# A decode backward kernel bound by 16 DMA engines: a fourth dV tile stored by 15 engines, and three wq loads moved to GpSimd's ring

## The chip, the cores and the metric

The kernel runs on 1 core of one Trainium2 chip. The metric is the device time of one execution in microseconds (us); lower is better. The kernel before took 404.36 us (median of three runs, 404.33 to 404.38). The profiled span is about 2 us shorter than the time.

The engines are called as in the profile: PE (matmul), DVE (vector), ACT (scalar), POOL (GpSimd), SP (sync). A DMA that SP issues goes into the hardware ring (q1 in the profile), one that GpSimd issues into the software ring (q0). Both are served by the same 16 DMA engines.

## The reference, cut to what matters

The outputs are the value and all gradients of a gated mix of one attention block for one token with a K and V cache, and one small MLP. What weighs is the caches: 32 heads, each with K and V of 4096 x 128 in bf16, 1 MB each, and their gradients, which are as large.

```python
def _A_ref(x, k_cache, v_cache, wq, wo):            # D = 640, H = 32, Sk = 4096, Dh = 128
    q = (x @ wq).reshape(B, Sq, H, Dh).transpose(0, 2, 1, 3)
    scores = jnp.einsum("bhqd,bhkd->bhqk", q, k_cache) * (Dh ** -0.5)
    p = _softmax(scores, axis=-1)
    o = jnp.einsum("bhqk,bhkd->bhqd", p, v_cache)
    return o.transpose(0, 2, 1, 3).reshape(B, Sq, H * Dh) @ wo
# [...] B: x @ w1 + b1, mish, @ w2
def reference(...):
    _out, _vjp = jax.vjp(_f, A_x, A_k_cache, A_v_cache, A_wq, A_wo, B_w1, B_b1, B_w2, gate_w)
    return (_out, *_vjp(grad_out))                   # dK and dV are 32 MB each
```

## The kernel before

It goes through the heads one after the other. K and V of a head are loaded three heads ahead, through SP's ring. Each head makes one dK tile and one dV tile of 1 MB, which GpSimd stores through its ring. One row of a tile is one partition: 32 x 128 elements of bf16, 8,192 bytes.

```python
    outs = ctx.enter_context(tc.tile_pool(name="outs", bufs=5))        # dK and dV tiles share 5 buffers
    tsb = ctx.enter_context(tc.tile_pool(name="tsb", bufs=4))
    wts = ctx.enter_context(tc.tile_pool(name="wts", bufs=2))
# [...]
    def ring(h):
        return nc.sync if h >= H - 2 else nc.gpsimd

    def load_k(h):
        if h < H:
            kts[h] = kv_in.tile([P, J, Dh], BF16, name="Kn", tag="Kn", bufs=KB)
            nc.sync.dma_start(kts[h][:], Kv[h])
# [...] load_v likewise
    def load_wq(w):
        if w < H // WG:
            wqs[w] = wts.tile([P, RC, WG * Dh], BF16, name="wq_g", tag="wq_g")
            nc.sync.dma_start(wqs[w][:], wq_v[:, :, w * WG * Dh:(w + 1) * WG * Dh])

    def load_wo(g):
        if g < NG:
            wos[g] = wts.tile([P, G, D], BF16, name="wo_g", tag="wo_g", bufs=3)
            nc.sync.dma_start(wos[g][:], wo_v[g])
# [...]
        def dwo():                                   # the gradient of wo is written over wo's own buffer
            for i in range(G):
                nc.vector.tensor_scalar(wos[g][:, i, :], da_bc[:], fs["o4"][:, i:i + 1], None, ALU.mult)
            (nc.sync if g == NG - 1 else nc.gpsimd).dma_start(dwo_v[g], wos[g][:])
# [...]
        if half == 1:                                # dv_half, after the outer product on DVE
            if h in (8, 17, 26):
                spread(h // 9, dVv[h], st["dV"])
            else:
                ring(h).dma_start(dVv[h], st["dV"][:])

    def spread(i, dst, t):
        src = t[:].rearrange("p j d -> p (j d)")
        out = dst.rearrange("p j d -> p (j d)")
        if i == 0:
            nc.gpsimd.inc_swdge_sem([], [], mode="reset_dge_cursor")
        for a, b in (((120, 125), (0, 120), (125, 128)), ((0, 14), (14, 119), (119, 128)), ((0, 8), (8, 128)))[i]:
            nc.gpsimd.dma_start(out[a:b, :], src[a:b, :], max_dma_last_dim=J * Dh)
# [...]
    for h in range(H):
        hh, g = h % G, h // G
        if hh == 3:
            load_wo(g + 2)
            if g % 2 == 0:
                load_wq(g // 2 + 1)
        load_k(h + 3)
        load_v(h + 3)
        period(h)
# [...]
```

`spread` is the device that the change uses once more. A store of 128 rows takes all 16 DMA engines, 8 rows each. A store of 120 rows takes 15. The odd pieces around it are there to choose which engine the 120 rows leave out.

## Time and profile before

| | before |
|---|---|
| time | 404.36 us (404.33 to 404.38) |
| moved by DMA | 164.93 MB |
| software ring, packets of 8,192 and of 4,096 bytes | 7,296 and 768 |
| DVE, PE, ACT busy | 75%, 74%, 44% of the span |
| the last DMA, dwq_l: fifteenth and last of its 16 landings | 398.93 and 401.22 us |

The first lines are from the page of the kernel before: span; the mean busy share of the 16 DMA engines and their GB/s in 40 equal slices of the span; the packet counts; each ring with packets, MB and share of the 16 engines' span; and the engine shares of the chain of waits that ended last.

```profile
span 402.3 us, 13607 instructions
...
DMA  7999999999999999999999999999999999999984
GB/s 283 418 416 406 419 424 420 418 422 424 422 422 418 423 414 403 425 423 423 422 421 424 423 422 419 418 426 425 421 423 425 421 424 417 425 420 417 424 368 189
DMA packets 28136, 164.93 MB, mean 410 GB/s; under 512 B 3164, under 2 KB 3868, under 8 KB 12204
...
q1 hardware_dynamic: 17136, 93.41, 56.3%
q0 software_dynamic: 10880, 70.64, 42.1%
q8 instruction: 46, 0.75, 0.7%
...
DVE 40%; DMA 27%; PE 20%; issue 5%; ACT 4%; POOL 0%; ACTq 0%; SPq 0%; POOLq 0%
DMA Kn<-in_A_k_cache_dram 22%; DVE dK_sb L612 10%; DVE dV_sb L612 9%; PE tr L587 8%; DVE junk L385 5%; DMA out_dram<-wo_g 4%; ACT tT L589 4%; PE sA L667 3%; DVE junk L288 3%; PE sA L596 3%; PE sB L720 2%; DVE junk L537 2%; DVE junk L494 1%; DMA vec_rows<-in_gate_w_dram 1%; DVE wo_g L374 1%
...
```

Read the row of DMA first. It is at 9, that is 90% or more, from the second slice to the last but two, at 414 to 426 GB/s in most. Compute engines are busy for three quarters. So the DMA engines bind, and the chain of waits does not say it: it gives DVE 40% and DMA 27%, since it follows what released each instruction and not which resource was full. The bandwidth agrees with what the Trainium skill ("DMA: Bandwidth & Descriptors", Bandwidth) measured for a load of 16 MB, 425 GB/s: most 8,192-byte packets here take 309 ns, and 16 engines at that pace move 424 GB/s.

These are the lines of the page on DMA issues (transfer, issuing sequencer, count, KB each, median us from issue to landing).

```profile
...
Kn<-in_A_k_cache_dram SPq DMA_DIRECT2D x32, 1024.0 KB, 23.7
...
out_dram<-dK_sb POOLq DMA_DIRECT2D x30, 1024.0 KB, 12.1
out_dram<-dV_sb POOLq DMA_DIRECT2D x27, 1024.0 KB, 12.0
wq_g<-in_A_wq_dram SPq DMA_DIRECT2D x4, 1280.0 KB, 19.6
...
out_dram<-wo_g POOLq DMA_DIRECT2D x7, 640.0 KB, 11.5
...
```

The stores through the software ring land 12 us after issue.

This is what SP's queue waited for (us in all, times, longest). L121 is the load of K. L136 is the load of wo.

```profile
...
SPq L121 <- PE sB L720: 182.6, 23, 19.6
SPq L136 <- DMA out_dram<-wo_g: 56.1, 5, 16.4
...
```

The first line is flow control: SP waits for a K buffer. The wait costs nothing as long as the DMA engines have other work, as the row of DMA shows here. In the second line, SP waits for the store of a wo_g buffer before it may load the next wo into it, 16.4 us at most.

The next lines are windows of the kernel before: start and end, length, busy us and instruction counts of the engines, the granted TensorE clock, the DMA share and GB/s.

```profile
...
core 0: us, PE busy (x) PEld busy (x) DVE busy (x) ACT busy (x) POOL busy (x), PEclk, DMA share, GB/s
...
280.00:290.00 10.00, 8.81 (x181) 7.91 (x177) 9.71 (x24) 5.89 (x15) 1.06 (x2) 1.00 1.02 423
290.00:300.00 10.00, 8.39 (x173) 7.51 (x171) 9.81 (x22) 5.24 (x14) 1.07 (x2) 1.00 1.01 424
...
380.00:390.00 10.00, 0.72 (x2) 0.27 (x2) 7.83 (x32) 0.26 (x1) 0.00 (x0) 0.50 0.96 401
...
```

And these are the lines on the wq loads and who waited for them (us, times).

```profile
...
L131 SPq DMA_DIRECT2D wq_g<-in_A_wq_dram x4: 412/466/548, 0.7 to 242.5; - x4
...
  PEld L278: 8.3, 2
  PE qc_ps L278: 8.1, 2
...
```

Before the end, the transfers of the kernel show who is late. Each transfer raises its semaphore 16 times, once per DMA engine. The times of these landings come from the semaphore records of the trace (us from the start of the span, in order; no engine is named there):

```
dK of the last head, second half, issued 381.96:
  388.50 388.75 388.82 388.97 389.10 389.81 392.58 393.89 394.10 394.78 395.31 395.43 395.51 395.61 395.68 | 398.09
dwq_l, the last DMA of the weights, issued 393.48:
  396.58 396.60 396.62 396.63 396.65 396.67 396.75 397.14 397.34 398.03 398.56 398.66 398.77 398.86 398.93 | 401.22
```

One engine is 2.3 us behind all others. It is called the straggler below.

### The profile page before, as it was taken

To read this page: it belongs to the slowest core of one execution; us is meant where nothing else is said; L and a number is where in the kernel's file an instruction comes from. 1 tells how busy PE (TensorE), PEld (TensorE's weight loads), DVE (VectorE), ACT (ScalarE), POOL (GpSimd) and SP (SyncE) were. 2 spreads that over 40 slices of the span, in tenths; PEclk is the share of its full clock that TensorE was granted. 3 is DMA by queue.
4 is the path that set the end of the run, shared out by engine and by line. 5 is a ranking of instruction groups with operands and counts; after the bars stand their busy time and mean duration, and the time that the engine had idled before them with its cause. 6 is when DMAs were issued, how large, how long until landed. Compare 5 with 4: busy or idle time off the path is not lost.

```text
span 402.3 us, 13607 instructions
## 1 busy us (share of the span) xinstructions
PE 298.5 (74%) x5872; PEld 270.1 (67%) x5872; DVE 303.1 (75%) x791; ACT 177.4 (44%) x411; POOL 45.6 (11%) x92
## 2 busy tenths in 40 slices
PE   0688898669888788978877989719887888888200
PEld 0587787668778677868766878618776777777200
DVE  3338666646599999987669799845999997899850
ACT  1355555325454555546523556505554455545000
POOL 0001111010112111111101112100110111111000
PEclk9999999857999999989988899957999999999655
DMA  7999999999999999999999999999999999999984
GB/s 283 418 416 406 419 424 420 418 422 424 422 422 418 423 414 403 425 423 423 422 421 424 423 422 419 418 426 425 421 423 425 421 424 417 425 420 417 424 368 189
DMA packets 28136, 164.93 MB, mean 410 GB/s; under 512 B 3164, under 2 KB 3868, under 8 KB 12204
## 3 DMA queue, kind: packets, MB, share of 16 engines
q1 hardware_dynamic: 17136, 93.41, 56.3%
q0 software_dynamic: 10880, 70.64, 42.1%
q8 instruction: 46, 0.75, 0.7%
q14 instruction: 14, 0.11, 0.1%
q10 hardware_dynamic: 60, 0.01, 0.0%
HBM read 82.03 MB, written 82.03 MB: 408 GB/s over the span
## 4 chain that ended last, share of the span: by engine, by line
DVE 40%; DMA 27%; PE 20%; issue 5%; ACT 4%; POOL 0%; ACTq 0%; SPq 0%; POOLq 0%
DMA Kn<-in_A_k_cache_dram 22%; DVE dK_sb L612 10%; DVE dV_sb L612 9%; PE tr L587 8%; DVE junk L385 5%; DMA out_dram<-wo_g 4%; ACT tT L589 4%; PE sA L667 3%; DVE junk L288 3%; PE sA L596 3%; PE sB L720 2%; DVE junk L537 2%; DVE junk L494 1%; DMA vec_rows<-in_gate_w_dram 1%; DVE wo_g L374 1%
## 5 line engine op out<-in xcount | busy, mean ns | idle before, releaser
L589 ACT COPY tT<-tr 128x512 f32<-128x512 f32 x256 | 142.5, 588 | 137.7 <-PE tr L587 136.9
L596 PEld LDWEIGHTS <-tT 128*128 128x128 bf16 x2048 | 79.8, 98 | 40.1 <-ACT tT L589 34.6
L587 PE MATMUL tr<-ident_f,Kn 128*128 128x128 f32 x512 | 81.9, 298 | 12.6 <-DMA Kn<-in_A_k_cache_dram 12.6
L612 DVE TENSOR_TENSOR dV_sb<-p_bf,qd 128x2048 bf16<-128x2048 bf16 x64 | 78.0, 1218 | 0.3 <-issue 0.3
L612 DVE TENSOR_TENSOR dK_sb<-ds_bf,qd 128x2048 bf16<-128x2048 bf16 x64 | 77.6, 1214 | 0.0
L587 PE MATMUL tr<-ident_f,Vn 128*128 128x128 f32 x512 | 74.3, 281 | 0.0
L587 PEld LDWEIGHTS tr<-ident_f,Kn 128*128 128x128 f32 x512 | 61.2, 152 | 13.9 <-issue 13.9
L596 PE MATMUL sA<-qd,tT 128*128 128x48 bf16 x1024 | 48.9, 187 | 23.8 <-ACT dq_all L725 12.7
L587 PEld LDWEIGHTS tr<-ident_f,Vn 128*128 128x128 f32 x512 | 57.4, 144 | 0.0
L596 PE MATMUL sB<-qd,tT 128*128 128x48 bf16 x1024 | 46.1, 183 | 0.0
L667 PEld LDWEIGHTS <-Vn 128*128 128x128 bf16 x1024 | 30.2, 96 | 10.4 <-issue 10.4
L667 PE MATMUL sA<-e_bf,Vn 128*128 128x48 bf16 x1024 | 30.7, 183 | 7.6 <-DVE zs L687 6.0
L720 PE MATMUL sB<-ds_bf,Kn 128*128 128x48 bf16 x1024 | 32.5, 186 | 1.4 <-DVE ds_bf L709 1.4
L629 POOL DMA_DIRECT2D out_dram<-dK_sb x30 | 17.2, 574 | 143.6 <-DVE rz L689 90.1
L671 DVE TENSOR_REDUCE m<-sA 128x1 f32<-128x32 f32 x32 | 6.0, 189 | 35.2 <-PE sA L596 28.5
L720 PEld LDWEIGHTS <-Kn 128*128 128x128 bf16 x1024 | 29.8, 98 | 1.6 <-issue 1.6
L642 POOL DMA_DIRECT2D out_dram<-dV_sb x27 | 14.6, 541 | 139.4 <-DVE dV_sb L612 53.3
L288 DVE SCALAR_TENSOR_TENSOR junk<-wo_g,da_bc 128x640 bf16<-128x640 bf16 x32 | 26.2, 820 | 1.7 <-ACT da_bc L229 1.1
L385 DVE SCALAR_TENSOR_TENSOR junk<-wq_g,dq_bc 128x1024 bf16<-128x1024 bf16 (+1 forms) x25 | 25.1, 1004 | 0.2
L691 ACT ACTIVATE p_bf<-e_bf,rz 128x64 bf16<-128x64 bf16 x32 | 11.1, 348 | 13.3 <-DVE rz L689 10.6
L707 DVE TENSOR_SCALAR_CACHE_REDUCE dj<-sB,rz 128x128 f32<-128x128 f32 x32 | 11.1, 346 | 7.5 <-PE sB L701 7.5
L698 DVE SCALAR_TENSOR_TENSOR pj<-sB,e_bf 128x32 f32<-128x32 f32 x32 | 6.1, 190 | 12.6 <-PE sB L596 12.4
(152 smaller groups left out, 273.6 us busy)
## 6 DMA issues: line engine op xcount, KB each, us to landing
Kn<-in_A_k_cache_dram SPq DMA_DIRECT2D x32, 1024.0 KB, 23.7
Vn<-in_A_v_cache_dram SPq DMA_DIRECT2D x32, 1024.0 KB, 28.2
out_dram<-dK_sb POOLq DMA_DIRECT2D x30, 1024.0 KB, 12.1
out_dram<-dV_sb POOLq DMA_DIRECT2D x27, 1024.0 KB, 12.0
wq_g<-in_A_wq_dram SPq DMA_DIRECT2D x4, 1280.0 KB, 19.6
wo_g<-in_A_wo_dram SPq DMA_DIRECT2D x8, 640.0 KB, 11.4
out_dram<-wo_g POOLq DMA_DIRECT2D x7, 640.0 KB, 11.5
out_dram<-dwq_t SPq DMA_DIRECT2D x4, 896.0 KB, 18.4
```

The source lines that it names most:

```text
L288: nc.vector.scalar_tensor_tensor(junk[:, 0:D], in0=wos[g][:, i, :], scalar=1.0, in1=da_bc[:], op0=ALU.mult, op1=ALU.mult, accum_out=gp["do ...
L385: nc.vector.scalar_tensor_tensor(junk[:, c0:c1], in0=wqs[w][:, rc, c0:c1], scalar=1.0, in1=dq_bc[:, w * WG * Dh + c0:w * WG * Dh + c1], op ...
L587: nc.tensor.transpose(tp[:, t, :], flat[:, k * P:(k + 1) * P], ident_f[:])
L589: nc.scalar.copy(sb[:].rearrange("p a b -> p (a b)"), tp[:].rearrange("p a b -> p (a b)"))
L596: nc.tensor.matmul(out[:, 2 * k:2 * k + W], lhsT=tb[:, t, par, :], rhs=vec[:, par, :].unsqueeze(1).to_broadcast([P, W // 2, 2]), start=(pa ...
L612: nc.vector.tensor_tensor(dst[:, a:b, :].rearrange("p j (a b) -> p j a b", b=2), col[:, a:b, :].unsqueeze(2).to_broadcast([P, n, Dh // 2, 2]),
L629: ring(h).dma_start(dKv[h], st["dK"][:])
L642: ring(h).dma_start(dVv[h], st["dV"][:])
L667: nc.tensor.matmul(O, lhsT=vts[h][:, j, :], rhs=st["e"][:, j:j + 1].to_broadcast([P, W]), start=(j == 0), stop=(j == J - 1))
L691: nc.scalar.activation(p_bf[:], e[:].unsqueeze(2).to_broadcast([P, J, 2]), ACT.Copy, scale=rz[:])
L707: nc.vector.tensor_scalar(dj[:], PT, rz[:], None, ALU.mult, ALU.add, accum_out=dd[:])
L720: nc.tensor.matmul(DQ, lhsT=kts[h][:, j, :], rhs=ds[:, j, 0:1].to_broadcast([P, W]), start=(j == 0), stop=(j == J - 1))
```

## The change

The intent: take one more dV tile off the slowest DMA engine (four spread tiles for three), and move three wq loads of 1.25 MB from SP's ring, where K and V queue behind them, to GpSimd's.

```diff
     def load_wq(w):
         if w < H // WG:
             wqs[w] = wts.tile([P, RC, WG * Dh], BF16, name="wq_g", tag="wq_g")
-            nc.sync.dma_start(wqs[w][:], wq_v[:, :, w * WG * Dh:(w + 1) * WG * Dh])
+            (nc.gpsimd if w else nc.sync).dma_start(wqs[w][:], wq_v[:, :, w * WG * Dh:(w + 1) * WG * Dh])
@@ dv_half
-            if h in (8, 17, 26):
-                spread(h // 9, dVv[h], st["dV"])
+            if h % 7 == 5 and h < H - 3:
+                spread(h // 7, dVv[h], st["dV"])
@@ spread
-        if i == 0:
+        if i % 3 == 0:
             nc.gpsimd.inc_swdge_sem([], [], mode="reset_dge_cursor")
-        for a, b in (((120, 125), (0, 120), (125, 128)), ((0, 14), (14, 119), (119, 128)), ((0, 8), (8, 128)))[i]:
+        for a, b in (((120, 125), (0, 120), (125, 128)), ((0, 14), (14, 119), (119, 128)), ((0, 8), (8, 128)))[i % 3]:
```

The spread tiles are now those of heads 5, 12, 19 and 26.

## The prediction

> **What bounds the kernel.** The 16 DMA engines. The 40-slice view has 420 to 425 GB/s in most slices; the table of windows gives a DMA share of 1.01 to 1.03 from 10 to 380 us. The page counts 164.93 MB; an 8,192-byte packet takes 309 ns, so 16 engines move 424 GB/s and need 389 us. Compute ends at 388.8 us, the span at 402.3.
>
> **Which engine.** The semaphore records show 16 landings per transfer, which show one engine's lag without its name. One is alone at the end: the last dK half lands at 388.5 (first), 394.1 (ninth), 395.7 (fifteenth) and 398.1 us (last); dwq_l at 396.6, 397.3, 398.9 and 401.2. Instruction fetch (46 packets of 16 KB, about 1 us each, one every 7 to 8 us) looks like its burden. Spread stores already relieve it: before the third (328 us) it is 4.3 to 4.8 us behind the fifteenth, after it 1.7.
>
> The Trainium skill ("DMA: Bandwidth & Descriptors", Why a DMA increments its semaphore by 16 and not by 1) says a software-ring transfer uses the largest k up to 16 that divides its partitions, on consecutive engines from a cursor. By that, 120 rows take 15 engines, and the pieces 5/120/3, 14/105/9, 8/120 all skip engine 4 with their big piece. The packet counts of before agree with the pieces (768 packets of 4,096 bytes for three tiles); no view names the engine.
>
> **What the change does.**
> 1. Four spread tiles (heads 5, 12, 19, 26) for three (8, 17, 26). The added one is of the 5/120/3 form: engine 4 carries 2 rows for 8, estimate 8 x 309 - 4 x 159 = 1.8 us less. Engines that get 9 rows in 4,096-byte packets gain 18 x 159 - 8 x 309 = 0.4 us. Two more issues on GpSimd (0.6 us each, 11% busy) and a cursor reset (18 ns): nothing.
> 2. Three wq loads (1.25 MB each) move from SP's ring to GpSimd's. Bytes, packets (640 of 2,048 bytes) and engines stay; the same page ("Issuing engines are not separate DMA queues") says rings share the 16 engines. Effects: K and V behind them on SP's ring come about 3 us earlier (1.25 MB at 424 GB/s), and wq itself lands after perhaps 12 to 15 us instead of 19.6 (dK and dV take 12 there), which should shorten PE's waits for wq (8.1 us in two). Neither is critical: the DMA engines have a backlog there.
>
> **Critical path.** Only the straggler's 1.8 us. Its last landing goes from 401.2 to about 399.4; the fifteenth goes from 398.9 to 399.0 to 399.3: they nearly meet. wo_g and dwq_l, issued at 391.3 and 393.5 after landings of the straggler (dwq_t at 393.4), go out about 2 us earlier. Time: 404.36 - 1.9 = 402.4 us; 401.2 to 403.8. Faster by over 2% (under 396.3): 0.02; within: 0.97; slower: 0.01.
>
> **Right if:** bytes and GB/s in mid-run unchanged; 1,024 packets of 4,096 bytes on the software ring instead of 768; gap of last to fifteenth landing at the end under 1 us instead of 2.3; PE's wait for wq falls.
>
> **Wrong if:** another engine is the straggler, or the cursor stands elsewhere (no gain, or 1 to 2 us slower); wq's 640 rows through software descriptors delay the stores behind them; the straggler had idle time, so that relief isn't time; ring order changes what waits at the end.

## The result, and the profile after

The changed kernel took 403.12 us (median of five runs: 403.73, 402.78, 402.68, 403.12, 403.42). The kernel before, five runs on the same chip, took 404.15 to 404.38. The ratio is 0.9974, with a 95% interval of 0.996 to 0.9988. (A ratio is the mean time of one kernel's runs over the mean of the other's in the same rounds, so it is not quite the ratio of the quoted medians.) The gain is about 1.05 us of the 1.9 predicted. The profiled run was the slowest of the five, 403.73 us.

The page of the changed kernel, the same lines:

```profile
span 401.8 us, 13610 instructions
...
DMA  8999999999999999999999999999999999999995
GB/s 285 420 415 399 420 423 408 423 422 421 417 415 425 423 422 412 423 424 420 423 419 422 424 421 422 414 422 425 415 399 423 421 422 420 424 421 416 423 410 213
DMA packets 27400, 164.93 MB, mean 410 GB/s; under 512 B 3260, under 2 KB 3964, under 8 KB 11596
...
q1 hardware_dynamic: 15168, 89.48, 54.0%
q0 software_dynamic: 12112, 74.57, 44.7%
q8 instruction: 46, 0.75, 0.7%
...
DVE 42%; DMA 25%; PE 19%; ACT 6%; issue 4%; POOL 0%; ACTq 0%; DVEq 0%; POOLq 0%
DVE dK_sb L612 11%; DVE dV_sb L612 9%; DMA out_dram<-dV_sb 9%; DMA out_dram<-dK_sb 8%; DMA wq_g<-in_A_wq_dram 7%; PE tr L587 6%; DVE junk L385 5%; ACT tT L589 5%; PE sA L667 4%; DVE junk L288 3%; PE sA L596 3%; PE sB L720 2%; DVE wo_g L374 1%; DMA vec_rows<-in_gate_w_dram 1%; DVE dj L707 1%
...
```

The bytes and the mean of 410 GB/s are as before. Two things differ. The last slices carry more (410 and 213 GB/s for 368 and 189): the engines end closer together. One slice in the middle, the thirtieth, at 291 to 301 us, fell to 399. The shares of the chain of waits changed much (K loads with 22% have gone, dV and dK stores with 17% have come) while the time hardly moved: it names other waits, no other limit. The ring counts fit the edit: q1 lost 1,968 packets, three loads of 640 and 48 semaphore writes; q0 gained 1,232, which are 960 for wq (320 each), 128 for the tile whose 128 rows now go in two packets each, and 144 of 4 bytes (48 semaphore writes of wq and 96 of the tile, explained below).

```profile
...
Kn<-in_A_k_cache_dram SPq DMA_DIRECT2D x32, 1024.0 KB, 21.2
...
out_dram<-dK_sb POOLq DMA_DIRECT2D x30, 1024.0 KB, 18.9
out_dram<-dV_sb POOLq DMA_DIRECT2D x26, 1024.0 KB, 18.9
...
out_dram<-wo_g POOLq DMA_DIRECT2D x7, 640.0 KB, 20.1
wq_g<-in_A_wq_dram POOLq DMA_DIRECT2D x3, 1280.0 KB, 27.1
...
```

The stores of whole dK and dV tiles and of wo_g through the software ring now land 19 to 20 us after issue, not 12. The three moved wq loads took 19.7, 27.1 and 29.5 us (semaphore records), for 37.0, 19.6 and 24.1 before: on the whole neither sooner nor later.

```profile
...
SPq L121 <- PE sB L720: 138.6, 18, 16.5
SPq L136 <- DMA out_dram<-wo_g: 106.0, 5, 24.8
...
```

SP's queue waits twice as long for wo's store buffer: 106.0 us, longest 24.8. The store in the longest wait was issued at 273.1 us and landed at 293.3. The third wq load, issued at 230.2, had landed at 259.7 by then; the store stood in the software ring behind dK and dV stores that were late themselves.

```profile
...
280.00:290.00 10.00, 5.32 (x105) 4.77 (x105) 8.01 (x20) 3.69 (x11) 0.87 (x3) 0.96 1.01 422
290.00:300.00 10.00, 9.17 (x141) 8.64 (x139) 8.36 (x19) 3.94 (x9) 0.85 (x2) 0.69 0.97 390
...
380.00:390.00 10.00, 0.72 (x2) 0.27 (x2) 7.83 (x32) 0.26 (x1) 0.00 (x0) 0.50 1.01 424
...
```

From 290 to 300 us the DMA engines moved 390 GB/s for 424 before: a hole of about 0.3 MB (34 GB/s x 10 us), about 0.8 us of all 16 engines. In the last window shown they moved 424 for 401.

```profile
...
L131 POOL DMA_DIRECT2D wq_g<-in_A_wq_dram x3: 901/901/901, 50.0 to 230.2; - x3
...
  PEld L278: 6.0, 2
  PE qc_ps L278: 5.8, 2
...
```

PE's wait for wq fell from 8.1 to 5.8 us. (GpSimd waited for wq too: the same view has one wait of 8.2 us at L531 and one of 7.1 us at L629 that ended with a wq load.) K and V, which no longer stand behind wq, land sooner after issue, as the page's first line on issues shows for K: 21.2 us for 23.7. The landings at the end, from the semaphore records:

```
dwq_l, issued 392.83:
  396.01 396.02 396.02 396.05 396.06 396.16 396.40 397.85 398.00 399.04 399.13 399.25 399.27 399.30 399.56 | 400.56
```

The straggler is now 1.0 us behind the fifteenth, as intended, and the fifteenth is 0.6 us later than before.

### Following each packet to its engine

The profile has one record for every packet, with ring, size, start and end, but names no engine. The engine can be worked out: on one engine the record of a packet starts 3 to 4 ns before that of the packet before it ends, each ring is served in order, and every transfer has to end with 16 landings at known times. Chaining all 28,000 packets this way gives 16 chains. Where two engines switch in the same nanosecond two chains can be swapped, so single packets are uncertain. The straggler's chain is not, since the spread stores mark it.

What marks it is this: an engine that a piece leaves out still gets packets, of 4 bytes and 9 ns each, as many as each engine that takes part has data packets. The page itself can be used to confirm it: each spread row goes as two packets of 4,096 bytes. By the rule of the Trainium skill ("DMA: Bandwidth & Descriptors", Why a DMA increments its semaphore by 16 and not by 1), 5, 120 and 3 rows take 5, 15 and 3 engines, with 2, 16 and 2 data packets each. That is 11 x 2 + 1 x 16 + 13 x 2 = 64 filler packets, and two more DMAs with 16 semaphore packets each are 32: 96 small packets for one such tile. The same sum gives 64 for the form 14/105/9 and 48 for 8/120. The page's count of packets under 512 bytes says 3,164 with three tiles, 3,260 with four (+96), 2,956 with none (-208 = 96 + 64 + 48), and 3,372 with six (+208): exact each time. So the rule holds in this trace.

In the kernel before, exactly one chain has runs of 18, 16 and 18 such small packets in a row at the three spread tiles. It moved 9.918 MB, the others 10.08 to 10.11 (the sums leave out some 2.7 MB of the two rings, about what moved in the first 10 us), and it is the one that ended last, at 400.88 us. By the same rule it is engine 4, if the reset puts the cursor at engine 0. No run here shows that it does, so the number is a name given by this assumption; that the pieces all leave out one and the same engine, and that this engine is the last one, is what the chains show. In the changed kernel it has runs of 18, 16, 18 and 18.

| straggler, us | packets at their usual length | longer than usual | gaps | its last packet ends |
|---|---|---|---|---|
| before | 378.3 | 18.8 | 0.7 | 400.9 |
| after | 376.1 | 20.1 | 0.7 | 400.2 |

"Usual length" is 309, 196 and 159 ns for 8,192, 5,120 and 4,096 bytes. All other engines are longer than usual by 1 to 4 us in sum before and 3 to 6 after. The straggler has nearly no gaps: it works all the time, and about one in four of its packets of 8,192 bytes takes 335 to 384 ns, loads and stores alike, while those of most other engines stay at 309.

### The profile page after: what moved, and what is told of

Its sections match the earlier page's. It is cut to its first block, busy times and chain, and to the rows that moved or that the text cites. A ratio compares the mean times of both kernels' runs of the same rounds, so it can differ in the third digit from the quotient of the medians. Undisturbed runs are those within 1.5% of the kernel's fastest.

```text
span 401.8 us, 13610 instructions
## 1 busy us (share of the span) xinstructions
PE 299.1 (74%) x5872; PEld 271.2 (67%) x5872; DVE 303.1 (75%) x791; ACT 178.1 (44%) x411; POOL 49.9 (12%) x97
## 2 busy tenths in 40 slices
DMA packets 27400, 164.93 MB, mean 410 GB/s; under 512 B 3260, under 2 KB 3964, under 8 KB 11596
## 4 chain that ended last, share of the span: by engine, by line
DVE 42%; DMA 25%; PE 19%; ACT 6%; issue 4%; POOL 0%; ACTq 0%; DVEq 0%; POOLq 0%
DVE dK_sb L612 11%; DVE dV_sb L612 9%; DMA out_dram<-dV_sb 9%; DMA out_dram<-dK_sb 8%; DMA wq_g<-in_A_wq_dram 7%; PE tr L587 6%; DVE junk L385 5%; ACT tT L589 5%; PE sA L667 4%; DVE junk L288 3%; PE sA L596 3%; PE sB L720 2%; DVE wo_g L374 1%; DMA vec_rows<-in_gate_w_dram 1%; DVE dj L707 1%
## 5 line engine op out<-in xcount | busy, mean ns | idle before, releaser
L587 PE MATMUL tr<-ident_f,Kn 128*128 128x128 f32 x512 | 80.1, 293 | 0.0
L587 PE MATMUL tr<-ident_f,Vn 128*128 128x128 f32 x512 | 76.3, 286 | 0.0
L587 PEld LDWEIGHTS tr<-ident_f,Vn 128*128 128x128 f32 x512 | 59.4, 147 | 0.0
L629 POOL DMA_DIRECT2D out_dram<-dK_sb x30 | 17.2, 575 | 134.5 <-DVE rz L689 86.7
L701 PE MATMUL sB<-ident_f,part 128*128 128x128 f32 x32 | 10.5, 330 | 4.2 <-DVE pj L698 4.0
## 6 DMA issues: line engine op xcount, KB each, us to landing
Kn<-in_A_k_cache_dram SPq DMA_DIRECT2D x32, 1024.0 KB, 21.2
out_dram<-dK_sb POOLq DMA_DIRECT2D x30, 1024.0 KB, 18.9
out_dram<-dV_sb POOLq DMA_DIRECT2D x26, 1024.0 KB, 18.9
out_dram<-wo_g POOLq DMA_DIRECT2D x7, 640.0 KB, 20.1
wq_g<-in_A_wq_dram POOLq DMA_DIRECT2D x3, 1280.0 KB, 27.1
```

Of the source, the lines that this page charges most:

```text
L587: nc.tensor.transpose(tp[:, t, :], flat[:, k * P:(k + 1) * P], ident_f[:])
L629: ring(h).dma_start(dKv[h], st["dK"][:])
L701: nc.tensor.transpose(PT, part[:].to_broadcast([P, P]), ident_f[:])
```

## The experiments

Twelve kernels were run. All outputs are right. All edits are against the kernel before. Each experiment's theories are told in words beside it; a letter in an expectation stands for one of them. Runs of one call shared the runs of the kernel before: medians 404.09 (e1 to e4), 404.20 (e5 to e8), 404.19 (e9 to e11), 404.22 (e12).

| kernel | spread tiles | wq ring | median us (range) | ratio to before, 95% interval |
|---|---|---|---|---|
| before | 3 | SP | 404.1 to 404.4 | 1 |
| after | 4 | GpSimd | 403.12 (402.68 to 403.73) | 0.9974 (0.996 to 0.9988) |
| e1_four_tiles | 4 | SP | 402.89 (402.31 to 403.40) | 0.9975 (0.9963 to 0.9988) |
| e2_wq_only | 3 | GpSimd | 404.90 (404.71 to 405.02) | 1.0024 (1.0011 to 1.0036) |
| e3_no_spread | 0 | SP | 410.18 (409.84 to 410.97) | 1.0158 (1.0144 to 1.0171) |
| e4_other_engine | 3, another engine left out | SP | 411.12 (410.55 to 411.35) | 1.0176 (1.0162 to 1.019) |
| e5_five_tiles | 5 | SP | 401.98 (401.88 to 405.47) | 0.9958 (0.9933 to 0.9982) |
| e6_six_tiles | 6 | SP | 402.14 (402.01 to 402.18) | 0.9947 (0.9935 to 0.9959) |
| e7_four_tiles_other_heads | 4, other heads | SP | 402.71 (402.21 to 403.34) | 0.9963 (0.9951 to 0.9975) |
| e8_five_tiles_wq | 5 | GpSimd | 405.22 (404.49 to 406.42) | 1.0028 (1.0015 to 1.0041) |
| e9_changed_wo_late | 4, wo issued later | GpSimd | 405.80 (404.41 to 407.93) | 1.0045 (1.0022 to 1.0069) |
| e10_five_wq_wo_late | 5, wo issued later | GpSimd | 406.18 (403.94 to 406.92) | 1.0038 (1.0015 to 1.0061) |
| e11_five_wo_late | 5, wo issued later | SP | 404.91 (403.37 to 408.31) | 1.0031 (0.9997 to 1.0066) |
| e12_five_wq_wo_buffers | 5, four wo buffers | GpSimd | 404.76 (403.46 to 405.99) | 1.001 (0.9988 to 1.0032) |

### e1 and e2: each half of the change alone

The theory was that the fourth tile is the whole gain, by relief of the straggler, and the wq move is worth nothing. The rival was that the wq move has an effect of its own.

e1 has only the tile:

```diff
-            if h in (8, 17, 26):
-                spread(h // 9, dVv[h], st["dV"])
+            if h % 7 == 5 and h < H - 3:
+                spread(h // 7, dVv[h], st["dV"])
```

(with `i % 3` in `spread`, as in the change)

> Four spread tiles alone, wq loads left on SP's ring. Theories on record: R (relief): the gain is the straggling engine's lighter load, worked out as 1.8 us, and the wq move costs nothing; Q (queue): the gain comes from moving wq, the tile is neutral; RC (relief less cost): the tile gives its full 1.8 us and the wq move costs about 0.8 us of it, as dK and dV stores landed after 18.9 us instead of 12 and DVE waited for store buffers. Before is 404.3. R: 403.1 as the whole change. Q: 404.3. RC: 402.4 to 402.6, faster than the whole change; end gap of last to fifteenth landing under 1 us.

Measured: 402.89 us, ratio 0.9975. The fourth tile alone gives all that the whole change gives. The time lies between what R and RC foresaw; the gap of last to fifteenth landing was 1.50 us in the profiled run (400.53 and 399.03), not under 1.

e2 has only the wq move:

```diff
-            nc.sync.dma_start(wqs[w][:], wq_v[:, :, w * WG * Dh:(w + 1) * WG * Dh])
+            (nc.gpsimd if w else nc.sync).dma_start(wqs[w][:], wq_v[:, :, w * WG * Dh:(w + 1) * WG * Dh])
```

> The wq loads on GpSimd's ring alone, three spread tiles at heads 8, 17, 26 as before. R: 404.3, unchanged. Q: 403.1. RC: 404.8 to 405.4, slower than before by 0.5 to 1 us; wq lands after more than 20 us; dK and dV stores land after 15 to 19 us instead of 12.

Measured: 404.90 us, ratio 1.0024, its interval above 1. The move alone is a loss of 1.0 us, as RC foresaw, and the dK and dV stores landed after 20.7 to 20.8 us (15 to 19 foreseen). On top of four tiles it costs 0.2 us between the medians (403.12 and 402.89), which the runs cannot tell from nothing. Whether the move truly costs less with four tiles than with three stays open: the two intervals, of 0.0013 to 0.0014 either way, leave about 0.8 us of uncertainty in the difference between the changed kernel and e1.

### e3 and e4: is it that one engine?

e3 spreads no tile. If three spread tiles relieve the straggler by what their packets say, the kernel must lose about 6 us. e4 also cuts three dV tiles into 120 and 8 rows, but resets the cursor each time and sends the 120 rows first, so that by the rule cited above (and a reset to engine 0) another engine, engine 15, is left out. If cutting a store helped by itself, or the slow engine were 15, e4 would be as fast as before. If only relief of engine 4 helps, e4 is as slow as e3.

```diff
e3:
-            if h in (8, 17, 26):
+            if False:
e4:
-        if i == 0:
-            nc.gpsimd.inc_swdge_sem([], [], mode="reset_dge_cursor")
-        for a, b in (((120, 125), (0, 120), (125, 128)), ((0, 14), (14, 119), (119, 128)), ((0, 8), (8, 128)))[i]:
+        nc.gpsimd.inc_swdge_sem([], [], mode="reset_dge_cursor")
+        for a, b in ((0, 120), (120, 128)):
```

> Before with no spread tile at all: all dV tiles stored by all 16 engines. Relief theories (R, RC): the straggler carries 3 tiles' relief more, 1.83 + 1.83 + 2.15 = 5.8 us by packets (8 of 309 ns less its own 4 or 2 of 159 ns), so 410.1 us (409 to 411) and a last landing 6 to 8 us behind the fifteenth at the end. Q: no more than 1 us slower than before.

> Before with its three spread tiles cut as rows 0 to 120 and 120 to 128, with the cursor reset each time: by the skill's rule the big piece takes engines 0 to 14 and leaves out engine 15, and the 8 rows go to 15 and 0 to 6, so engine 4 gets 9 rows in 4,096-byte packets, 0.36 us more than a plain tile, instead of 1 or 2. If engine 4 is the straggler and the cursor rule holds: 410.1 + 1.1 = 411.2 us (410 to 412), slower even than no spread tile. If it doesn't matter which engine is spared, or the straggler is 15: 404.3 or less.

Measured: 410.18 us and 411.12 us. Relief of one certain engine is worth 6.1 us for three tiles; relief of the other one, engine 15 by the rule, is worth nothing (0.9 us slower than no cutting, which is near the scatter). The chain of the straggler has no run of fillers in either. In both, the straggler ends alone: the second dK half of the last head lands at 395.16 (fifteenth) and 404.48 (last) in e3, and at 395.24 and 404.65 in e4. The Trainium skill ("DMA: Bandwidth & Descriptors", Latency and other measured facts) says engines 7 and 15 are usually slower than the rest; here, by the same page's cursor rule and if the reset means engine 0, it is engine 4.

The chains of before and e3 also settle what does not burden the straggler. Instruction fetch (46 packets of 16 KB, about 1 us each) falls on eight other engines in turn, about six fetches each, and shows there as 5 to 6 us of gaps. The straggler's chain has 0.4 us of gaps in all, and its own packets are 19.5 us too long. So it is not the fetch.

### e5, e6 and e7: more tiles, other heads

If the straggler were the only limit, the fifth and sixth tile would each give as much as the fourth. If a second limit lies close behind, the gain ends. e7 keeps four tiles, the three of before and head 22, to see if the place of the tiles matters.

```diff
e5:
+            if h % 6 == 4 and h < H - 3:              # heads 4, 10, 16, 22, 28
+                spread(h // 6, dVv[h], st["dV"])
e6:
+            if h % 5 == 3 and h < H - 3:              # heads 3, 8, 13, 18, 23, 28
+                spread(h // 5, dVv[h], st["dV"])
e7:
+            if h in (8, 17, 22, 26):
+                spread((8, 17, 22, 26).index(h), dVv[h], st["dV"])
```

> Five spread tiles (heads 4, 10, 16, 22, 28), wq on SP's ring. Theory F (floor): the fourth tile gave 1.0 us only as its relief was over-counted (18 more 4-byte packets of 9 ns on the spared engine: 1.65 us, not 1.83) and as that engine's packets ran 0.6 us longer in sum; a fifth gives the same again until the eight engines that fetch instructions (last at 398.6 us before, 0.3 to 0.4 us more with the extra rows) are last: about 1.9 us under before, 402.0 to 402.4 if before is 404.1, spared engine no longer last by more than 0.5 us. Rival S (saturation): the fourth tile met something else that ends the program; the fifth gives nothing, 402.9 to 403.2.

> Six spread tiles (heads 3, 8, 13, 18, 23, 28), wq on SP's ring. F: the spared engine ends about 1.5 us ahead of the fetching ones, which have 0.3 to 0.7 us more than before; no better than five tiles, 402.0 to 402.7. S: as four and five tiles. If every tile still gave 1 us: 401.1.

> Four spread tiles at heads 8, 17, 22, 26 instead of 5, 12, 19, 26, wq on SP's ring. If only the spared engine's total counts (F): as the four tiles of before, 0.8 to 1.3 us under before. If the places of the tiles matter (relief that comes early is lost): nearer the full 1.65 us, 402.3 or less.

Measured: e5 401.88 to 402.02 us in five runs and 405.47 in the sixth, which was the profiled one; e6 402.01 to 402.18 in all five; e7 402.71. So the heads matter little, the fifth tile gives 0.7 us (against e7) to 0.9 us (against e1) more than four, and the sixth nothing. e6 is the best kernel by its ratio, 0.9947, 2.1 us under the kernel before, and it is also under the changed kernel and e1 (403.12 and 402.89 us).

The page of e6 has the same bytes and a shorter span:

```profile
span 400.2 us, 13615 instructions
...
GB/s 288 418 417 400 422 424 415 419 427 420 422 425 419 423 421 418 422 426 421 422 423 422 422 425 409 415 425 424 424 422 421 425 422 423 422 417 419 426 397 233
DMA packets 28728, 164.93 MB, mean 412 GB/s; under 512 B 3372, under 2 KB 4076, under 8 KB 13180
...
```

Its straggler ended at 395.3 us, before the eight engines with the instruction fetches, which ended at up to 398.8. dwq_l has its fifteenth landing at 399.12 and its last at 399.15: no engine is alone any more. So the next floor is those eight engines, and the straggler has 3.5 us to spare.

e5's outlying run has a late engine again, with dwq_l's last landing at 402.61 for 399.09 of the fifteenth. At 350 to 360 us the packets in the software ring took 330 ns for 8,192 bytes and 174 for 4,096, against 309 and 159, and the slice at 353 to 363 us moved 391 GB/s. It was one run in six, and why is not known.

### e8: the wq move once the straggler is no longer last

With five tiles or more the straggler is no longer alone at the end. If the wq move is only harmless because the straggler is last, it must cost now.

```diff
+            (nc.gpsimd if w else nc.sync).dma_start(wqs[w][:], wq_v[:, :, w * WG * Dh:(w + 1) * WG * Dh])
# and the five tiles of e5
```

> Five spread tiles and the wq loads on GpSimd's ring. The wq move alone made the time 1.0 us longer with three tiles (spared engine's packets 0.74 us longer in sum, 0.54 us saved by 4,096-byte packets) and nothing or 0.2 us with four. If its cost sits on the spared engine only, it costs nothing here, where other engines are last: within 0.3 us of five tiles alone. If it delays stores or loads for all engines: 0.5 to 1 us slower than five tiles alone.

Measured: 405.22 us. The move costs 3.2 us with five tiles (401.98 without it), more than either theory foresaw. It had cost 1.0 us in e2 as well, where the straggler is last, so a late straggler alone does not make it harmless. The windows of e8 show the hole again, and deeper than in the changed kernel:

```profile
...
280.00:290.00 10.00, 6.54 (x102) 5.74 (x100) 6.62 (x16) 4.32 (x11) 1.68 (x3) 0.89 1.02 422
290.00:300.00 10.00, 8.49 (x166) 7.70 (x166) 9.50 (x22) 4.88 (x11) 1.33 (x2) 0.94 0.98 356
...
```

356 GB/s at 290 to 300 us is about 0.7 MB less than 424 would be, or 1.6 us of all engines, if none of it is made up later. The packets of the fetching engines were also longer: 4 to 6 us too long in sum in e8, against 2.4 to 3.0 in e6. By that, an estimate, some 2 of the 3.2 us are longer packets on the engines that end last. The theory put to the test next was that the hole is the cost.

### e9, e10 and e11: take the hole away by a later wo load

The theory (called W from here on): the cost is SP's queue standing at the wo load, whose buffer waits for a store that is stuck in the software ring, with all K and V loads behind it. In the changed kernel SP issued K and V at 267.7 and 268.1 us, and the next ones at 293.8, since the wo load waited until 293.3. The hardware ring was empty from 285 to 293 us. If wo is issued after K and V of the same head, the hole should close and the time with it.

```diff
         if hh == 3:
-            load_wo(g + 2)
             if g % 2 == 0:
                 load_wq(g // 2 + 1)
         load_k(h + 3)
         load_v(h + 3)
+        if hh == 3:
+            load_wo(g + 2)
# e9: on the changed kernel; e10: on e8; e11, the control: on e5
```

> The changed kernel with each wo load issued after the K and V loads of its period, not before them. Theory W (wait in SP's queue): with wq on the software ring the dwo store before it lands after 20 instead of 11.5 us, the wo load waits for that store's buffer (25 us in one wait, 268 to 293 us), the K and V loads behind it wait too, and the hardware ring is empty from 285 to 293 us. Here 290 to 300 us should be at 415 GB/s or more instead of 387 and 392, and the loads K and V near 270 to 290 us go out in time. Time: the spared engine was last and not idle there, so little is expected: 402.3 to 403.0. Rival L (the longer packets alone): the hole closes or not, time as the changed kernel, 403.0 to 403.3.

> Five spread tiles, wq on GpSimd's ring, wo loads after K and V. With five tiles the other engines are last, and the wq move made it 405.2 instead of 402.0. W: with the wait out of the way of K and V, 401.8 to 402.6, and no hole under 400 GB/s between 285 and 300 us. L: still 404 or more.

> Control: five spread tiles, wq on SP's ring, wo loads after K and V. That kernel had no hole (418 to 425 GB/s from 280 to 305 us), so both theories: 401.8 to 402.3, as five tiles alone. If it is faster by as much as e10, the order of the loads is a gain of its own and not a cure of the wq move.

Measured: 405.80, 406.18 and 404.91 us. All three are slower, and the control, for which both theories foresaw 401.8 to 402.3, lost 2.9 us too though it has no wq move. The hole at 290 to 300 us did close (416 GB/s in e9, 414 in e10), but other dips came (376 at 275 to 280 in e9, 341 at 300 to 305 in e10). The edit brought a delay of its own, and that it is the cost is argued and not shown: wo now arrives late. In e11 DVE waits for it, as the waits of DVE show (us in all, times, longest):

```profile
...
DVE junk L288 <- DMA wo_g<-in_A_wo_dram: 26.3, 4, 9.7
...
```

The slices of e11 have new dips, of 403 GB/s in the twenty-eighth and 394 and 404 near the end. So this trio says nothing of W. Without the control it would have been read as evidence against W.

### e12: take the wait away by a fourth wo buffer

Here the order stays, and the wo load finds a free buffer. (Four buffers did not fit; the buffers of the transposed tiles went from four to three to make room.) W says 401.6 to 402.6 us. The rival, called L, says that the wait is a symptom, and that the loads in the software ring cost by themselves: 404.5 to 405.5.

```diff
-    tsb = ctx.enter_context(tc.tile_pool(name="tsb", bufs=4))
+    tsb = ctx.enter_context(tc.tile_pool(name="tsb", bufs=3))
-            wos[g] = wts.tile([P, G, D], BF16, name="wo_g", tag="wo_g", bufs=3)
+            wos[g] = wts.tile([P, G, D], BF16, name="wo_g", tag="wo_g", bufs=4)
# and the wq move and five tiles of e8; dwq_l uses the same four buffers
```

> Five spread tiles, wq on GpSimd's ring, wo loads in their old place but with four buffers instead of three, so that a wo load waits for the dwo store of two groups ago and not of the last one (to make room, the transposes' copies have three buffers instead of four, which should cost nothing as PE is not the limit). The same kernel with three wo buffers took 405.2, five tiles with wq on SP's ring 402.0. Theory W (the wq move costs time as it delays the dwo store for which SP's queue then waits, K and V loads behind it): no wait of 25 us at the wo loads, no window under 410 GB/s between 285 and 305 us, 401.6 to 402.6 us. Rival L (longer packets or the fuller software ring itself): 404.5 to 405.5, hole or no hole. In between, both have a share.

Measured: 404.76 us (403.46 to 405.99). The wait is gone: in SP's waits the only line left of L136 is the one of 3.2 us for wq, and the K loads wait for their own buffers instead (first line).

```profile
...
SPq L121 <- PE sB L720: 247.8, 27, 16.0
...
SPq L136 <- DMA wq_g<-in_A_wq_dram: 3.2, 1, 3.2
...
```

The hole is gone too, and another dip has come later:

```profile
...
280.00:290.00 10.00, 8.26 (x170) 7.41 (x168) 9.81 (x24) 5.34 (x15) 2.45 (x4) 1.00 1.01 420
290.00:300.00 10.00, 8.34 (x172) 7.40 (x168) 9.81 (x22) 5.24 (x13) 1.14 (x2) 1.00 1.02 421
...
360.00:370.00 10.00, 7.98 (x163) 7.31 (x164) 9.02 (x19) 4.67 (x12) 2.09 (x3) 1.00 1.02 383
...
```

421 GB/s at 290 to 300 us for 356 in e8, but 383 at 360 to 370. The time fell by 0.5 us, no more than the runs scatter. So L's number held and W's did not: the hole is real, but with it filled, and a dip elsewhere, the loss is still there. In the dip of e12 the software ring's packets took 333 ns (8,192 bytes) and 210 (4,096); in e8's hole, at 296 to 300 us, 384 and 240. In the dip of e12 nearly only stores were in flight; in e8's hole loads were too (at 296 to 300 us, 80 packets of a wo load and 12 of K, beside 136 of stores). Stores alone do not explain it: the changed kernel moved 419 GB/s at 284 to 290 us with no load in flight, its 8,192-byte packets at 311 ns. Why packets get longer, no run shows. One rival was not tested: the deep dips of e5's outlier, e8, e10, e11 and e12 each hold packets of a spread tile (head 22 or 28), and no run keeps that tile away from them. A dip does not need it, since e3, which spreads no tile, has one too (339 GB/s at 280 to 285 us). One weakness: e12 has a transposed buffer less than e8, and no control had that alone.

## Why the prediction was right or wrong

**The time.** The class and the range were right: 403.12 us lies in 401.2 to 403.8, above the point of 402.4. The gain was 1.05 us for 1.9.

**The bound, and the mechanism.** Right. The DMA engines bind, one of them is last, and the change works only through that engine. e3 and e4 show it by time (6.1 us for three tiles on the right engine, nothing on another), e1 shows that the tile is all of the gain. The gap of last to fifteenth landing went from 2.29 to 0.99 us ("under 1 us" was said). The packet patterns confirm the cursor rule and that the big piece skips that engine.

**The step that failed on size: "estimate 8 x 309 - 4 x 159 = 1.8 us less".** In e1 the straggler's packets at usual length went down by 1.52 us (378.29 to 376.77). The estimate left out 18 small packets of 9 ns each, 0.16 us: 16 fillers of the piece that skips the engine and two more semaphore writes. The remaining 0.15 us was not itemised. In the profiled run of e1 the same engine was also 0.6 us slower in the rest of its packets (19.36 us too long for 18.77). This sum differs from run to run without a pattern, 18.2 to 20.1 us over the profiled runs of before, after, e1 to e4 and e7, so a relief of 1.5 us shows as 1.0 (e1) or 1.5 (e7, 0.9963) in the time.

**The step that failed on cause: "Instruction fetch (46 packets of 16 KB, about 1 us each, one every 7 to 8 us) looks like its burden".** Wrong. The fetches fall on eight other engines. The straggler's packets are themselves longer, over the whole run. The prediction had argued it from the count of fetches; nothing it had read tied one fetch to the late engine. Why its packets are longer stays open. The error did no harm to the time, since the relief does not depend on the cause. It hid that those eight engines are the next floor: the fifth tile ends the gain (e5, e6).

**The step that failed on wq: "Bytes, packets (640 of 2,048 bytes) and engines stay".** Packets do not stay. In the software ring each load went as 320 packets of 4,096 bytes. So that ring's count of such packets was 1,984 and not the 1,024 predicted: 768 + 256 from the tile + 960 from wq. The straggler was 0.7 us shorter at usual length (376.77 in e1, 376.07 after), of which 0.54 us follow from these packets (40 of 84 ns against 20 of 159, three times, at the lengths of the trace); longer packets took it back (19.36 to 20.10).

**"wq itself lands after perhaps 12 to 15 us instead of 19.6".** Wrong for all three: 19.7, 27.1 and 29.5 us. The 19.6 itself was one landing of three (37.0, 19.6 and 24.1). The 12 us of dK and dV was taken as a property of the ring, but it changes with what stands in the queue: three transfers of 1.25 MB more, and the stores land after 18.9 us (20.7 in e2, which has only the move).

**"Neither is critical: the DMA engines have a backlog there".** The conclusion held for the whole change, where the move cost 0.2 us, which the runs cannot tell from nothing; in part that was luck. It does not hold of the move as such: 1.0 us in e2, with the straggler last there too, and 3.2 us in e8. The straggler was not idle after the change (0.67 us of gaps in all) while the others idled up to 2 us in the hole, but e2 shows that this alone does not make the move free; why it is nearly free with four tiles stays open. And the reason given failed. The backlog was not there: the hardware ring ran dry from 285 to 293 us. "Bytes and GB/s in mid-run unchanged" failed with it, 390 for 424. The prediction did list this among what would make it wrong, that wq's rows "delay the stores behind them".

**What PE gained.** Its wait for wq did fall, from 8.1 to 5.8 us, and it is worth nothing in the time, as said.

**The end.** The last landing was foreseen at 399.4 and came at 400.56 in the profiled run; the fifteenth was foreseen at 399.0 to 399.3 and came at 399.56. dwq_l went out 0.65 us earlier, not 2.

**What stays open.** Why one engine's packets are longer; why packets of all engines get longer in the dips; what the 3.2 us of the move in e8 consist of (e12, without the wait, was 0.5 us faster, no more than the scatter); and whether the wq move costs less with four tiles than with three.

## What to carry to other kernels

When DMA engines bind, look at the 16 landings of the last transfers: one late engine is worth relieving with a store of 120 rows, and the gain ends where the second group of engines stands, so add tiles until the last landings meet (here five to six tiles and 2.1 us, not four). Moving loads to another ring moves them into that ring's queue: price what stands behind them, above all a store whose buffer a load in the first ring waits for. Test each half of a change alone, since here one half gave the whole gain, and the other was a loss (1.0 us with three tiles, 3.2 with five) that the whole change did not show.

## What the Trainium skill lacked or had wrong

- "DMA: Bandwidth & Descriptors", Why a DMA increments its semaphore by 16 and not by 1: the rule for the number of engines held in every count here, and the pieces of each spread tile left out one and the same chain, as the cursor rule has it. It does not say that an engine left out by a software-ring piece gets as many packets of 4 bytes (9 ns each) as the others get data packets, 16 for a piece of 120 rows in packets of 4,096 bytes. They took, with two semaphore writes, 0.16 us off the relief per tile (an estimate, 18 x 9 ns).
- "DMA: Bandwidth & Descriptors", Issuing engines are not separate DMA queues: it says that issuing from several engines only saves time on the sequencer. Here moving three loads from SP to GpSimd changed the landing of the stores in that ring (12.0 to 18.9 us), and cost 1.0 us with three spread tiles and 3.2 us with five.
- "DMA: Bandwidth & Descriptors", Latency and other measured facts: it says engines 7 and 15 are usually slower. Here the slow one is engine 4 by the same page's cursor rule, if the reset puts the cursor at engine 0 (no page and no run here says so), with 18 to 20 us of longer packets over the run, and sparing the engine that is 15 by the same rule gained nothing (411.12 us for 410.18 without any sparing).
- No page has which DMA engines fetch instructions: here 46 fetches of 16 KB and about 1 us fell on eight engines in turn, not on the slow one, with 5 to 6 us of gaps on each, and these engines are the floor once the slow one is relieved (398.8 us for 395.3 in the kernel with six tiles).
